# Second layer of a fused attention and MoE kernel: its first two chunks placed inside the w_out product, its second product two chunks behind, the last group ending with chunk 0

## Chip, cores and metric

The kernel runs on one core of a Trainium2 chip. The metric is the device time of that core in microseconds (us); lower is better. Engines are named TensorE (PE in the profile; PEld is its weight load), VectorE (DVE), ScalarE (ACT), GpSimd (POOL) and SyncE (SP, which issues DMA transfers).

## Reference

The attention part gives x, 2304 tokens of 512 values. Two layers follow. All inputs come in 64-bit floats.

```python
a = phi - np.max(phi, axis=2, keepdims=True); a = np.exp(a)
a = a / (np.sum(a, axis=2, keepdims=True) + 1e-09)
k_m = np.einsum('bhsm,bhsd->bhmd', a, k); v_m = np.einsum('bhsm,bhsd->bhmd', a, v)
scores = scale * np.matmul(q, k_m.transpose(0, 1, 3, 2))
attn = softmax(scores)                 # max, exp, sum + 1e-09
x = np.matmul(attn, v_m)               # (4, 8, 576, 64) -> (2304, 512)

h = np.maximum(np.maximum(x @ w1, x @ w2), x @ w3)   # 512 -> 768
y = h @ w_out                                        # 768 -> 512

h = y @ w_in                                         # 512 -> 2048
g = np.maximum(h, 0.0) + np.log1p(np.exp(-np.abs(h)))
out = g @ w_out2                                     # 2048 -> 512
```

## The kernel before

Every product is made of three matmuls in reduced-precision 32-bit floats: a value is split into a high part, cast by ScalarE (L160), and a rest, value minus high part, by VectorE or GpSimd (L168). The 64-bit inputs are converted on the chip by the class `Conv`: ScalarE scales the upper word (L196 with Prelu, called "slope", or L198 with Copy, called "bits"), VectorE shifts (L203) and joins the lower word (L204) and, for "bits" alone, puts the sign back (L207); then ScalarE casts the high part and GpSimd makes the rest (L168). Between load and conversion stand two buffers `raw` and two buffers `cg`.

The first layer runs in two passes of 1152 tokens (three chunks of 384). `phase_a(pp)` makes h, `phase_o(pp)` the product with w_out: 18 steps, one per chunk cc and block j of 128 hidden values, in the order 5, 0, 1, 2, 3, 4. A step is 12 matmuls (L685 to L687, 128x384) into four PSUM banks, out of a ring of six (`psm`). `hsplit` splits h two steps ahead, into a ring of four buffers: the high part hh on ScalarE, the rest hlo on the engine that a table names, which is VectorE for two of the 18 steps in the second pass and GpSimd for the others. After a chunk's last step, ScalarE casts the four banks to yb (L160) and VectorE makes their rests (L168); that frees the banks. So the next chunk finds two banks free and waits for the other two.

During `phase_o(1)` the weight blocks of the second layer are loaded and converted by `w2_steps`, blocks 0 to 3 by "slope". The second layer runs over 96 steps: four groups of four blocks of 128 hidden values, in each group six chunks ck of 384 tokens, in each chunk the four blocks. A step n has `m2in` (12 matmuls, L918, into one of two `pst` banks), `soft1` (e on VectorE L924, L by ScalarE's Softplus L926, m on VectorE L928), `soft2` (high part gh on ScalarE L160, rest gl on GpSimd L168) and `m2out` (9 matmuls, L961, 128x512, into three `acc` banks). At a chunk's last block, the sums go to o: copied in group 0, added on VectorE (L974) in later groups. In the last group the rows of o are stored by SyncE (L133), where a tile of 128 tokens is cut into up to three pieces by the token order of the output.

From the start of the second pass on, a scheduler fixes the order on each engine: it takes the instructions in the order of the program text and lets one that is ready sooner go ahead. `m2out(n-1)` is written behind `m2in(n)`. Two lines, L673 in `hsplit` and one in `dma`, set who makes a rest and where transfers are issued:

```python
        rest(C["hl"][6 * cc + j], lo, src, hi)
            with tc.issue_after(LOADED["plan"]):
```

`issue_after(i)` orders what is traced under it behind instruction i where both are on the same engine.

## Time and profile before

| | us |
|---|---|
| median of 3 runs | 723.62 (723.2 to 723.75) |
| the profiled execution | 723.56 |
| its span | 721.7 |
| w_out product of the second pass, about | 265 to 307 |
| second layer, steady stretch | 316.22 to 712.36 |
| last stretch | 712.36 to 721.75 |

The times that the rows give are counted from the span's start. In a timeline's row stand the start, the duration, engine, line, operation, output<-input, count, and in brackets how long the engine idled before it and which instruction released it. A row can hold several instructions run one behind the other. PEclk is the granted clock of TensorE as a share of full speed. A matmul's duration holds its way through the array, so the distance of two starts is the price of one.

### The profile page before, as it was taken

Reading aid. Unit: us, or ns where it says so; the run is one execution under the profiler, and the core shown is the slowest. Engines: PE = TensorE matmul, PEld = TensorE weight load, DVE = VectorE, ACT = ScalarE, POOL = GpSimd, SP = SyncE. Lnnn points to the kernel's source line nnn. Section 1 sums busy time; section 2 is a strip of 40 time slices with the busy share of each in tenths; the row PEclk is TensorE's granted clock in tenths of the full one; section 3 lists DMA queues with packets and bytes.
Section 4 is the critical chain, followed back from the end, with each engine's and each line's share of the span. In section 5 each row is a group of like instructions: output and inputs, shape, how many; then the busy total and the mean of one; then the engine's idle time right before and its main releaser. Section 6 shows DMA issues by size and latency. Waiting matters only on the chain. (4 is left out here: it accounts for less than half of the span.)

```text
span 721.7 us, 11376 instructions
## 1 busy us (share of the span) xinstructions
PE 683.8 (95%) x4216; PEld 606.2 (84%) x4216; DVE 416.9 (58%) x764; ACT 299.9 (42%) x640; POOL 269.8 (37%) x283
## 2 busy tenths in 40 slices
PE   4788999999889999989999999999999999999996
PEld 3475778988779999879989988998888989998984
DVE  4789787845799846842333784344873336333432
ACT  3556355565676625543233542223442224222221
POOL 2513053474493228712222542223542225212221
PEclk9799999999979999999999999999999999999999
DMA  9992996132162005410000240000330000011212
GB/s 240 268 271 77 245 286 196 64 120 76 51 198 91 1 2 161 131 59 1 0 1 1 87 132 15 1 0 19 105 111 1 1 1 0 1 45 44 69 47 61
DMA packets 57463, 59.19 MB, mean 82 GB/s; under 512 B 9792, under 2 KB 52288, under 8 KB 57408
## 3 DMA queue, kind: packets, MB, share of 16 engines
q1 hardware_dynamic: 57024, 58.34, 27.8%
q8 instruction: 33, 0.54, 0.3%
q10 hardware_dynamic: 384, 0.13, 0.1%
q14 instruction: 22, 0.18, 0.1%
HBM read 53.74 MB, written 4.72 MB: 81 GB/s over the span
## 5 line engine op out<-in xcount | busy, mean ns | idle before, releaser
L168 POOL TENSOR_TENSOR gl<-m,gh 128x384 fp32r<-128x384 f32 x96 | 101.0, 1054 | 255.0 <-ACT gh L160 238.6
L924 DVE TENSOR_SCALAR e<-pst 128x384 int32<-128x384 int32 x96 | 53.2, 555 | 135.5 <-PE pst L918 135.5
L926 ACT ACTIVATE L<-e 128x384 f32<-128x384 f32 x96 | 50.4, 525 | 185.5 <-DVE e L924 185.4
L961 PE MATMUL acc<-ol,gh 128*128 128x512 f32 x288 | 114.1, 396 | 0.0
L961 PE MATMUL acc<-oh,gh 128*128 128x512 f32 x288 | 113.6, 394 | 0.4 <-ACT gh L160 0.4
L918 PE MATMUL pst<-yb,ih 128*128 128x384 f32 x384 | 102.2, 337 | 0.0
L639 PE MATMUL psm<-ah,uh 128*128 128x288 f32 x288 | 88.6, 309 | 3.6 <-ACT ah L504 1.0
L639 PE MATMUL psm<-al,uh 128*128 128x288 f32 x288 | 86.9, 302 | 1.1 <-DVE al L168 1.0
L639 PE MATMUL psm<-ah,ul 128*128 128x288 f32 x288 | 86.2, 301 | 0.0
L928 DVE SCALAR_TENSOR_TENSOR m<-pst,L 128x384 f32<-128x384 f32 x96 | 53.4, 556 | 56.4 <-ACT L L926 56.4
L961 PE MATMUL acc<-oh,gl 128*128 128x512 f32 x288 | 82.8, 396 | 0.0
L160 ACT ACTIVATE gh<-m 128x384 fp32r<-128x384 f32 x96 | 50.0, 523 | 64.5 <-DVE m L928 63.2
L918 PEld LDWEIGHTS pst<-yb,ih 128*128 128x128 f32 x384 | 70.1, 188 | 3.5 <-DVE m L928 0.7
L918 PE MATMUL pst<-y0h,ih 128*128 128x384 f32 x192 | 65.7, 342 | 2.7 <-DVE m L928 2.6
L918 PE MATMUL pst<-y0l,ih 128*128 128x384 f32 x192 | 65.1, 339 | 0.0
L918 PE MATMUL pst<-y0h,il 128*128 128x384 f32 x192 | 65.1, 339 | 0.0
L918 PE MATMUL pst<-yb,il 128*128 128x384 f32 x192 | 64.4, 336 | 0.0
L639 PEld LDWEIGHTS psm<-ah,uh 128*128 128x128 f32 x288 | 55.3, 192 | 9.7 <-DVE h L649 2.6
L961 PEld LDWEIGHTS acc<-oh,gl 128*128 128x128 f32 x288 | 53.7, 188 | 11.3
L961 PEld LDWEIGHTS acc<-oh,gh 128*128 128x128 f32 x288 | 54.0, 188 | 10.2 <-ACT gh L160 0.9
L961 PEld LDWEIGHTS acc<-ol,gh 128*128 128x128 f32 x288 | 54.1, 188 | 9.1
L639 PEld LDWEIGHTS psm<-al,uh 128*128 128x128 f32 x288 | 55.8, 194 | 1.7 <-DVE al L168 1.7
(161 smaller groups left out, 1330.9 us busy)
## 6 DMA issues: line engine op xcount, KB each, us to landing
wraw<-in_moe_w_dram SPq DMA_DIRECT2D x66, 256.0 KB, 4.3
raw<-in_moe_w_in_dram SPq DMA_DIRECT2D x16, 512.0 KB, 3.7
raw<-in_moe_w_out_dram SPq DMA_DIRECT2D x16, 512.0 KB, 3.6
kvm<-in_k_dram SPq DMA_DIRECT2D x8, 512.0 KB, 7.7
kvm<-in_v_dram SPq DMA_DIRECT2D x8, 512.0 KB, 6.9
wor<-in_moe_w_out_dram SPq DMA_DIRECT2D x6, 512.0 KB, 4.1
ph<-in_phi_dram SPq DMA_DIRECT2D x8, 256.0 KB, 5.2
qn<-in_q_dram SPq DMA_DIRECT2D x4, 512.0 KB, 5.1
```

The costliest lines, as they stand in the source:

```text
L160: nc.scalar.activation(out=dst, in_=src, func=AF.Copy)
L168: return e.tensor_tensor(out=dst, in0=src, in1=hi, op=ALU.subtract)
L639: nc.tensor.matmul(x, l[:, t, ws], r[:, cs], start=(n == 0), stop=(n == 5))
L918: nc.tensor.matmul(hx, l[:, ds], r[:, cs], start=(n == 0), stop=(n == 3 * ND - 1))
L924: nc.vector.tensor_scalar(out=e.bitcast(I32), in0=hx.bitcast(I32), scalar1=0x7FFFFFFF, scalar2=None, op0=ALU.bitwise_and)
L926: nc.scalar.activation(out=L, in_=e, func=AF.Softplus, scale=-1.0)
L928: nc.vector.scalar_tensor_tensor(out=m, in0=hx, scalar=0.0, in1=L, op0=ALU.max, op1=ALU.add)
L961: nc.tensor.matmul(acc[0][t], l[:, t * P:(t + 1) * P], r, **kw)
```

## The change

- `hsplit` takes an engine: in pass 1 rests with cc + j odd are made by VectorE, the others by GpSimd, nine each.
- Blocks 2 and 3 of the second layer's weights are converted by "bits" in place of "slope", which adds four L207 steps on VectorE.
- The tiles of the softplus lie in a pool of their own; `m2in` and `soft1` of steps 0 and 1 are put at steps 10 and 12 of the w_out product, `soft2(0)` at step 12.
- `m2out(n-2)` is written behind `m2in(n)`.
- From step 2 on, loads are issued under `issue_after` of the last matmul of `m2in(2)`.
- The last group takes the chunks in the order 1 to 5, 0. In its last step the 128-token tiles go in the order of their number of pieces, the rest's matmuls between them; four stores follow, two on SyncE and two on ScalarE's queue.

```diff
-    def hsplit(cc, j):
+    def hsplit(cc, j, eng=None):
...
-        rest(C["hl"][6 * cc + j], lo, src, hi)
+        rest(eng or C["hl"][6 * cc + j], lo, src, hi)
...
+        eng = [None if pp == 0 else "dve" if (cc + j) % 2 else "pool" for cc, j in seq]
...
     for f in range(FG):
-        w2_steps(bg, 4 * f, f)
-    phase_o(1, bg)
...
+        w2_steps(bg, 4 * f, f, **({} if f < 2 else {"sgn": "bits"}))
+    s_p = pool(ctx, "soft", side="left")
...
+    seq = [(fg, ck, fi) for fg in range(NG2) for ck in [(x + fg // (NG2 - 1)) % (2 * NCH) for x in range(2 * NCH)]
+           for fi in range(FG)]
...
+    def front(n):
+        fg, ck, fi = seq[n]
+        hx, i = m2in(n, ck, fg * FG + fi)
+        soft1(n, hx)
+        return i
+
+    for n in range(2):
+        bg[10 + 2 * n].append(lambda n=n: front(n))
+    bg[12].append(lambda: soft2(0))
+    phase_o(1, bg)
...
-        for t in range(NTT):
+        ts, end = range(NTT), n == len(seq) - 1
+        if end:
+            ts = sorted(ts, key=lambda t: -len(rows(ck * CH + t * P)))
+        lows = []
+        for x, t in enumerate(ts):
             mm(gh, oh, t, start=(fi == 0), stop=False)
             mm(gh, ol, t, start=False, stop=False)
-        for t in range(NTT):
-            mm(gl, oh, t, start=False, stop=last)
+            if end and x:
+                lows.append(ts[x - 1])
+                mm(gl, oh, ts[x - 1], start=False, stop=True)
+        for t in ts:
+            if t not in lows:
+                mm(gl, oh, t, start=False, stop=last)
...
-                    for p0, n, r0, st in rows(ck * CH + t * P):
-                        dma(out=out[r0:r0 + (n - 1) * st + 1:st, :], in_=O[ck, t][p0:p0 + n])
...
+                    for x, (p0, k, r0, st) in enumerate(rows(ck * CH + t * P)):
+                        dma(nc.scalar if end and (x or t == 1) else nc.sync, out=out[r0:r0 + (k - 1) * st + 1:st, :],
+                            in_=O[ck, t][p0:p0 + k])
...
-    for n, (fg, ck, fi) in enumerate(seq):
-        hx = m2in(n, ck, fg * FG + fi)
-        if n:
-            soft2(n - 1)
-        soft1(n, hx)
+    for n in range(2, len(seq) + 2):
+        if n < len(seq):
+            i = front(n)
+            if n == 2:
+                LOADED["plan"] = i
+        if n <= len(seq):
+            soft2(n - 1)
         for fn in bg.get(n, ()):
             fn()
-        if n:
-            m2out(n - 1)
-    soft2(len(seq) - 1)
-    m2out(len(seq) - 1)
+        m2out(n - 2)
```

In the changed kernel e is L919, L is L921, m is L923, `m2in` L913, `m2out` L976 and the stores L131.

**Where the second chunk's banks are freed.** On VectorE, before, the end of the conversion of block 4 (L204, L207) and the rests of yb for the second chunk's first two banks stand so:

```order
L204 SCALAR_TENSOR_TENSOR cg<-raw,cg 128x512
L203 TENSOR_SCALAR cg<-cg 128x512
L207 SCALAR_TENSOR_TENSOR cg<-raw,cg 128x512
L204 SCALAR_TENSOR_TENSOR cg<-raw,cg 128x512
L207 SCALAR_TENSOR_TENSOR cg<-raw,cg 128x512
L168 TENSOR_TENSOR yb_3486<-psm,yb 128x384
L203 TENSOR_SCALAR cg<-cg 128x512
L168 TENSOR_TENSOR yb_3488<-psm,yb 128x384
```

In the changed kernel the same place reads:

```order
L204 SCALAR_TENSOR_TENSOR cg<-raw,cg 128x512
L207 SCALAR_TENSOR_TENSOR cg<-raw,cg 128x512
L168 TENSOR_TENSOR hlo<-h,hh 128x384
L919 TENSOR_SCALAR e<-pst 128x384
L168 TENSOR_TENSOR yb_3486<-psm,yb 128x384
L203 TENSOR_SCALAR cg<-cg 128x512
L923 SCALAR_TENSOR_TENSOR m<-pst,L 128x384
L204 SCALAR_TENSOR_TENSOR cg<-raw,cg 128x512
L168 TENSOR_TENSOR yb_3488<-psm,yb 128x384
```

A rest of h and e of step 0 stand ahead of the first bank's rest, and m of step 0 with a whole L204 step between the first and the second.

On ScalarE, before, from block 4's cast oh to the four casts of yb (`yb_3485` is the first bank's):

```order
L160 ACTIVATE oh_3988<-cg_4138 128x512
L160 ACTIVATE yb_3485<-psm_3644 128x384
L198 ACTIVATE cg_4354<-raw_4286 128x512
L160 ACTIVATE yb_3487<-psm_3645 128x384
L160 ACTIVATE yb_3489<-psm_3646 128x384
L160 ACTIVATE hh_3820<-h_3057 128x384
L160 ACTIVATE yb_3491<-psm_3647 128x384
```

In the changed kernel:

```order
L160 ACTIVATE oh_3983<-cg_4133 128x512
L160 ACTIVATE yb_3485<-psm_3647 128x384
L198 ACTIVATE cg_4352<-raw_4281 128x512
L921 ACT_TABLE_LOAD
L921 ACTIVATE L_3774<-e_3772 128x384
L160 ACTIVATE yb_3487<-psm_3648 128x384
L160 ACTIVATE yb_3489<-psm_3649 128x384
L160 ACTIVATE hh_3867<-h_3057 128x384
```

The table load and L of step 0 stand between the casts of the first and the second bank.

**Where the second layer's second product begins.** On TensorE, before, the end of the first `m2out` (`acc`) and what follows it:

```order
L961 MATMUL acc_3953<-oh,gh 128x512
L961 MATMUL acc_3953<-ol,gh 128x512
L961 MATMUL acc_3951<-oh,gl 128x512
L961 MATMUL acc_3952<-oh,gl 128x512
L961 MATMUL acc_3953<-oh,gl 128x512
L918 MATMUL pst<-y0h_2739,ih 128x384
L918 MATMUL pst<-y0h_2739,il 128x384
L918 MATMUL pst<-y0l_2740,ih 128x384
L918 MATMUL pst<-y0h_2866,ih 128x384
```

In the changed kernel:

```order
L976 MATMUL acc_3991<-oh,gh 128x512
L976 MATMUL acc_3991<-ol,gh 128x512
L976 MATMUL acc_3989<-oh,gl 128x512
L976 MATMUL acc_3990<-oh,gl 128x512
L976 MATMUL acc_3991<-oh,gl 128x512
L976 MATMUL acc_3989<-oh,gh 128x512
L976 MATMUL acc_3989<-ol,gh 128x512
L976 MATMUL acc_3990<-oh,gh 128x512
L976 MATMUL acc_3990<-ol,gh 128x512
```

Two blocks of `m2out` follow each other, where one stood, since one more `m2in` has gone ahead of them.

**The last stores.** On SyncE, before, the last seven stores, all of the last chunk, and the end:

```order
L133 DMA out_dram<-o_4830 64x512
L133 DMA out_dram<-o_4830 32x512 x2
L133 DMA out_dram<-o_4832 96x512
L133 DMA out_dram<-o_4832 32x512
L133 DMA out_dram<-o_4834 96x512
L133 DMA out_dram<-o_4834 32x512
L1022 UNCONDITIONAL_BRANCH
```

In the changed kernel the last rows of SyncE, of which two stores are the last chunk's, and then those of ScalarE:

```order
L131 DMA out_dram<-o_4866 96x512
L131 DMA out_dram<-o_4866 32x512
L131 DMA out_dram<-o_4108 32x512
L131 DMA out_dram<-o_4104 128x512
L1043 UNCONDITIONAL_BRANCH
```

```order
L921 ACTIVATE L<-e 128x384
L160 ACTIVATE gh<-m 128x384
L131 DMA out_dram<-o_4108 96x512
L131 DMA out_dram<-o_4106 128x512
L1043 UNCONDITIONAL_BRANCH
```

Of the last chunk's four stores two stand on either queue, two of them whole tiles of 128 rows.

## Rows read from the trace of the kernel before

**Rows 1.** Page, busy us (share of the span) x instructions of each engine.

```profile
PE 683.8 (95%) x4216; PEld 606.2 (84%) x4216; DVE 416.9 (58%) x764; ACT 299.9 (42%) x640; POOL 269.8 (37%) x283
```

**Rows 2.** Windows: us, busy PE PEld DVE ACT POOL, PEclk, DMA, GB/s.

```profile
268.76:295.54 26.78, 25.91 (x146) 24.75 (x144) 20.30 (x23) 14.33 (x28) 22.16 (x18) 1.00 0.44 137
286.01:298.44 12.43, 10.58 (x55) 8.97 (x54) 8.47 (x11) 7.11 (x15) 10.34 (x8) 1.00 0.50 158
298.44:316.22 17.78, 15.60 (x77) 14.86 (x78) 13.05 (x21) 9.21 (x17) 8.73 (x7) 0.90 0.40 122
312.54:316.05 3.51, 3.51 (x12) 3.51 (x13) 0.97 (x2) 1.49 (x3) 2.01 (x2) 0.53 0.15 61
316.22:712.36 396.14, 395.59 (x1972) 355.14 (x1971) 178.68 (x299) 125.54 (x238) 125.02 (x113) 1.00 0.11 32
712.36:721.75 9.39, 2.37 (x10) 1.61 (x9) 1.88 (x3) 0.40 (x1) 1.02 (x1) 0.83 0.29 84
```

**Rows 3.** Chain of waits, second layer: start us, us, engine, tile, line, count.

```profile
428.68 2.10 PE acc L961 x9
430.78 3.54 PE pst L918 x20
```

**Rows 4.** TensorE in 265 to 300: waits (total, times, longest), then a weight load.

```profile
PE psm L687 <- POOL hlo L168: 1.8, 3, 0.9
...
298.44 0.19 PEld L685 LDWEIGHTS psm<-hh,wo 128*128 128x128 f32 x1 [0.40 <-DVE yb L168]
```

**Rows 5.** TensorE's timeline behind the first softplus: start us, us, ..., [idle <-releaser].

```profile
312.54 0.69 PE L918 MATMUL pst<-y0h,ih 128*128 128x384 f32 x1 [2.17 <-DVE m L928]
```

**Rows 6.** Timelines of VectorE in the second pass, and GpSimd at one place.

```profile
219.33 0.54 DVE L168 TENSOR_TENSOR hlo<-h,hh 128x384 fp32r<-128x384 f32 x1
...
289.51 1.36 DVE L168 TENSOR_TENSOR hlo<-h,hh 128x384 fp32r<-128x384 f32 x1
...
291.74 0.68 DVE L207 SCALAR_TENSOR_TENSOR cg<-raw,cg 128x512 int32<-128x512 int32 x1
...
293.87 1.67 DVE L207 SCALAR_TENSOR_TENSOR cg<-raw,cg 128x512 int32<-128x512 int32 x1
296.61 0.56 DVE L168 TENSOR_TENSOR yb<-psm,yb 128x384 fp32r<-128x384 f32 x1 [1.07 <-ACT yb L160]
...
289.27 1.19 POOL L168 TENSOR_TENSOR hlo<-h,hh 128x384 fp32r<-128x384 f32 x1
```

**Rows 7.** ScalarE's timeline, from the second chunk's banks to the first softplus.

```profile
290.52 0.67 ACT L198 ACTIVATE cg<-raw 128x512 f32<-128x512 f32 x1 [1.28 <-POOL hlo L168]
...
295.57 0.63 ACT L160 ACTIVATE oh<-cg 128x512 fp32r<-128x512 f32 x1 [2.08 <-DVE cg L207]
...
297.04 0.86 ACT L160 ACTIVATE yb<-psm 128x384 fp32r<-128x384 f32 x2
...
309.32 1.28 ACT L926 ACT_TABLE_LOAD   x1
311.12 0.52 ACT L926 ACTIVATE L<-e 128x384 f32<-128x384 f32 x1 [0.52 <-DVE e L924]
```

**Rows 8.** Page, the costliest groups: the last step of the softplus.

```profile
L928 DVE SCALAR_TENSOR_TENSOR m<-pst,L 128x384 f32<-128x384 f32 x96 | 53.4, 556 | 56.4 <-ACT L L926 56.4
```

**Rows 9.** TensorE's timeline at the end of the kernel.

```profile
711.50 0.86 PE L961 MATMUL acc<-oh,gl 128*128 128x512 f32 x3
712.81 0.50 PE L961 MATMUL acc<-oh,gh 128*128 128x512 f32 x1 [0.44 <-ACT gh L160]
```

**Rows 10.** End of the kernel: timelines of VectorE and SyncE, and store landings.

```profile
714.74 1.88 DVE L974 TENSOR_TENSOR o<-o,acc 128x512 f32<-128x512 f32 x3 [2.60 <-PE acc L961]
...
715.46 3.45 SPq L133 DMA_DIRECT2D out_dram<-o  x7
...
out_dram<-o SPq DMA_DIRECT2D x2, 192.0 KB, 2.3
```

More of the change, by code (lines that the diff above doesn't have):

```diff
@@ L748, in phase_o @@
         seq = [(cc, jof(pp * NJ + x)) for cc in range(NCH) for x in range(NJ)]
-        hsplit(*seq[0])
-        hsplit(*seq[1])
+        eng = [None if pp == 0 else "dve" if (cc + j) % 2 else "pool" for cc, j in seq]
+        hsplit(*seq[0], eng[0])
+        hsplit(*seq[1], eng[1])
         main = []
         for n, a in enumerate(seq):
-            main.append(lambda a=a, n=n: (m1out(pp, *a), hsplit(*seq[n + 2]) if n + 2 < len(seq) else None))
+            main.append(lambda a=a, n=n: (m1out(pp, *a), hsplit(*seq[n + 2], eng[n + 2]) if n + 2 < len(seq) else None))
         run(main, bg)
@@ L895, in fused_kernel @@
     for f in range(FG):
-        w2_steps(bg, 4 * f, f)
-    phase_o(1, bg)
-    right.close()
-    psA_s.close()
-    b_p = pool(ctx, "bwork", side="right")
-    psx = pool(ctx, "psx", space=PSUM)
+        w2_steps(bg, 4 * f, f, **({} if f < 2 else {"sgn": "bits"}))
+    s_p = pool(ctx, "soft", side="left")
     G, acc, O = {}, {}, {}
@@ L917, in m2in @@
             for l, r in ((ih, yh), (il, yh), (ih, yl)):
-                nc.tensor.matmul(hx, l[:, ds], r[:, cs], start=(n == 0), stop=(n == 3 * ND - 1))
+                i = nc.tensor.matmul(hx, l[:, ds], r[:, cs], start=(n == 0), stop=(n == 3 * ND - 1))
                 n += 1
-        return hx
+        return hx, i.ins
     def soft1(n, hx):
-        e = b_p.tile([P, CH], F32, tag="e", name="e", bufs=2)
+        e = s_p.tile([P, CH], F32, tag="e", name="e", bufs=2)
         nc.vector.tensor_scalar(out=e.bitcast(I32), in0=hx.bitcast(I32), scalar1=0x7FFFFFFF, scalar2=None, op0=ALU.bitwise_and)
-        L = b_p.tile([P, CH], F32, tag="L", name="L", bufs=2)
+        L = s_p.tile([P, CH], F32, tag="L", name="L", bufs=2)
         nc.scalar.activation(out=L, in_=e, func=AF.Softplus, scale=-1.0)
-        m = b_p.tile([P, CH], F32, tag="m", name="m", bufs=2)
+        m = s_p.tile([P, CH], F32, tag="m", name="m", bufs=2)
         nc.vector.scalar_tensor_tensor(out=m, in0=hx, scalar=0.0, in1=L, op0=ALU.max, op1=ALU.add)
@@ L932, in soft2 @@
         m = G[n]
-        gh = b_p.tile([P, CH], F32R, tag="gh", name="gh", bufs=3)
-        gl = b_p.tile([P, CH], F32R, tag="gl", name="gl", bufs=3)
+        gh = s_p.tile([P, CH], F32R, tag="gh", name="gh", bufs=3)
+        gl = s_p.tile([P, CH], F32R, tag="gl", name="gl", bufs=3)
         cast("act", gh, m)
@@ L937, in soft2 @@
         G[n] = (gh, gl)
+    seq = [(fg, ck, fi) for fg in range(NG2) for ck in [(x + fg // (NG2 - 1)) % (2 * NCH) for x in range(2 * NCH)]
+           for fi in range(FG)]
+    GS = 2 * NCH * FG
+    def front(n):
[7 more added lines that the diff above has]
+    phase_o(1, bg)
+    right.close()
+    psA_s.close()
+    b_p = pool(ctx, "bwork", side="right")
+    psx = pool(ctx, "psx", space=PSUM)
     def rows(c0):
@@ L961, in mm @@
             nc.tensor.matmul(acc[0][t], l[:, t * P:(t + 1) * P], r, **kw)
-        for t in range(NTT):
+        ts, end = range(NTT), n == len(seq) - 1
[3 more added lines that the diff above has]
+        for x, t in enumerate(ts):
             mm(gh, oh, t, start=(fi == 0), stop=False)
             mm(gh, ol, t, start=False, stop=False)
-        for t in range(NTT):
-            mm(gl, oh, t, start=False, stop=last)
+            if end and x:
[4 more added lines that the diff above has]
+                mm(gl, oh, t, start=False, stop=last)
         if last:
-            for t in range(NTT):
+            for t in ts:
                 if fg == 0:
@@ L975, in m2out @@
                 if fg == NG2 - 1:
-                    for p0, n, r0, st in rows(ck * CH + t * P):
-                        dma(out=out[r0:r0 + (n - 1) * st + 1:st, :], in_=O[ck, t][p0:p0 + n])
-    seq = [(fg, ck, fi) for fg in range(NG2) for ck in range(2 * NCH) for fi in range(FG)]
-    GS = 2 * NCH * FG
+                    for x, (p0, k, r0, st) in enumerate(rows(ck * CH + t * P)):
+                        dma(nc.scalar if end and (x or t == 1) else nc.sync, out=out[r0:r0 + (k - 1) * st + 1:st, :],
+                            in_=O[ck, t][p0:p0 + k])
     bg = defaultdict(list)
```

## Prediction

> **What bounds the kernel now.** I read the busy shares first: TensorE is busy for 683.8 of 721.7 us, the next engine for 58% [rows 1]. So only what lets TensorE start a matmul earlier, or shortens what follows its last matmul, moves the time. The profiled execution took 723.56 us, its span 721.7; the median of the runs is 723.62. I count from 723.56.
>
> Next came the windows. In the steady stretch of the second layer, 316.22 to 712.36 us, TensorE is busy for 395.59 of 396.14 us at full granted clock [rows 2]. Nothing is to be had there. The change can act on two places: the w_out product of the second pass with the passage into the second layer (265 to 316 us), and the last 9 us.
>
> I then took the price of one matmul where nothing waits: 20 of the second layer's first product take 3.54 us, 0.176 each; 9 of its second take 2.10 us, 0.233 each [rows 3]. By that price 55 matmuls in 286.01 to 298.44 are 9.68 us of 12.43, so 2.75 us are lost there; 77 in 298.44 to 316.22 are 13.55 of 17.78, so 4.2 are lost there [rows 2]. The lines show where. In the product TensorE waits for the low rests of h on GpSimd (three waits, the longest 0.93 us) and, at 298.44, for a PSUM bank that the rests of yb on VectorE free [rows 4]. After the product it idles 2.17 us at 312.54, behind the first softplus, and the 12 matmuls that follow take 3.51 us at a granted clock of 0.53, the lower of the two levels (1.2 of 2.4 GHz): 1.4 us more than 12 x 0.176 [rows 2, 5].
>
> **The passage, with nothing late.** I set a fixed point: the fourth PSUM bank of the product's last chunk opening, 298.44 before. From it to the first matmul of the second layer's second product (316.22) there were 77 matmuls. In the new order there are 78: 54 of the product and 24 of m2in, since m2in(1) and most of m2in(0) have gone ahead of it. One m2in more than before is done by then, 12 x 0.176 = 2.11 us of work that need not be done later. So if the bank opens at X, the gain is 316.22 + 2.11 - X - 78 x 0.176 = 304.6 - X. Without any wait, X is 298.44, less the 2.75 lost, plus 16 m2in matmuls that move ahead of it (2.82), less 5 product matmuls that move behind it (0.88): 297.63. The gain would be 7.0 us. This is the upper bound, with the 2.17 idle, the low clock and the waits for GpSimd all gone.
>
> **When the bank opens.** The bank needs ScalarE's cast and VectorE's rest of yb. Both engines reach them after the second half of weight block 4. On VectorE that conversion's last step ended at 293.87 + 1.67 = 295.54 [rows 6]. The source queues the held loads behind a TensorE instruction, but the loads sit on SyncE, and in the new order the conversions of blocks 4 to 6 stand where they stood; I give the hold no effect, and this is where the change doesn't do what it says. From 268.76 to 295.54 VectorE is busy for 20.30 of 26.78 us, so 6.5 are idle [rows 2]. The change adds four more rests of h (0.54 us alone at 219.33, 1.36 at 289.51 beside GpSimd's row at 289.27) and four L207 steps of blocks 2 and 3, 0.68 to 1.67 each [rows 6]: 4 x 0.54 + 4 x 0.68 = 4.9 to 4 x 1.36 + 4 x 1.67 = 12.1. Against 6.5 idle that makes the conversion 0 to 5.6 late, but the idle lies in pieces, behind loads and ScalarE's steps, and not every added step meets one. Walking the ring of two raw tiles from load to ScalarE to VectorE gives about 1.0 later, with the row lengths nearer 0.68; I take 1.0 (296.5) and keep 0 to 3.
>
> From 296.5 on ScalarE does three steps, the cast of oh, that of yb for bank 1 and a cg step; before, they took from 295.57 to 297.04, 1.47 us [rows 7]. So they end at 298.0, bank 1's cast in their middle at about 297.4. Then, and this is new, the softplus table load stands between the first and the second yb cast: 1.28, and L(0) 0.52 [rows 7], to 299.85. VectorE adds m, 0.56 [rows 8], an L204 step taken at 0.68 like the L207 row, and the second yb rest, 0.56 [rows 6]: X = 301.7. Before, the same stretch from the conversion's end to the bank was 2.90; now it is 5.2. GpSimd is no part of it, and its load falls by eight rests. The gain is 304.6 - 301.7 = 2.9, of the 7.0. TensorE's waits for GpSimd and its 2.17 us are gone, and in their place it stands at the third bank (freed about 298.2, wanted at 295.5: 2.7 us) and again at the fourth (1.4).
>
> After an idle of 2.17 us the trace shows the clock at 0.53 for 3.51 us [rows 2, 5]. After an idle of 2.7 I expect the same once. Most falls on the 12 matmuls before the second wait, which it only shortens. I take 0.5 lost, bounds 0 and 2.8 (two such stretches). Small waits elsewhere, for the first chunk's rests behind an added L207 step, for the third chunk's behind block 6: 0.3, bounds 0 and 1. One of the nine rests goes into the phase ahead of the product; its 0.54 I count at 0, bounds -0.5 and 0.5. Passage: -2.9 + 0.5 + 0.3 = -2.1.
>
> The Trainium skill, "ScalarE: Activation LUTs", section "What ACT_TABLE_LOAD costs", counts a drain of 1380 ns beside the 1283 ns of a load. By it X would be 1.38 later and the time 1.4 us longer, about 720.9. The row at 311.12 [rows 7] doesn't show such a drain: L started 1.80 us after the load began, released by its own input.
>
> **Two chunks behind.** m2out(n-2) follows m2in(n), so TensorE has two blocks of work while a softplus runs. In the steady stretch the old order covers it but for 0.55 us in all (395.59 of 396.14 [rows 2]); I leave this at 0, bounds -0.5 and +1. At the end it counts. The block before the last ended 711.50 + 3 x 0.233 = 712.20, and the last began 712.81 [rows 9], behind gh. Now two blocks of 2.10 us stand over that chain: -0.6. The granted clock after it was 0.83 on average [rows 2]: -0.1.
>
> **The stores.** Before, VectorE's three last adds start at 714.74 and the seven stores on SyncE take 3.45 us to issue from 715.46 [rows 10], 0.49 each: the last starts at 718.42, and the window ends at 721.75 [rows 2]. Chunk 0 last needs four stores, on two queues, so the last is issued behind the third add, 714.74 + 1.88 = 716.62. With the same tail the gain is 721.75 - 718.42 - (721.75 - 716.65), thus 1.8. But the last store now is 256 KB and all four move at once; stores of 192 KB landed in 2.3 us. The same bytes in less time can cost up to 0.9. I take -1.3, bounds -0.9 and -1.8. ScalarE has nothing else to do by then, so its two issues are free.
>
> **Sum.** 723.56 - 2.1 - 0.6 - 0.1 - 1.3 = 719.46, said as 719.4.
>
> **Rivals.**
> - The forecast, the wait moves to the second chunk's banks: 717 to 721.5. For it: on both engines the order puts the load, L and m ahead of the second rest. Chance 0.55.
> - All hidden: VectorE's idle takes the added steps in full, and the conversion of block 4 even ends 2 us earlier than before, since ScalarE's cg step at 290.52, which waited 1.28 behind a rest of h on GpSimd [rows 7], starts sooner. X near 298.7 gives 5.9, the end 2.0: 715.7 or, at the bound of 7.0, 714.5. For it: the 6.5 us of idle. Against it: the load's 1.28 stands on the path all the same. Chance 0.17.
> - Only the end pays: the conversion ends at 299.4, X is 304.6, and the passage gives nothing and costs one low-clock stretch of 1.4: 723.56 + 1.4 - 2.0 = 723.0; with half of that delay 721.6. Chance 0.20.
> - Slower: VectorE becomes the bound of the product. If the rests take 1.36 and the L207 steps 1.67 [rows 6], the conversion ends 5.6 late, X is 306.3, the passage loses 1.7 and two low-clock stretches 2.8, the end gives 2.0: 726.1. It decides from X = 305.3, a conversion ending at 300.1. For it: the 1.36 row beside a busy GpSimd. Against it: GpSimd was busy 22.16 of 26.78 us [rows 2] and loses rests, so fewer meet. Chance 0.08.
>
> On the last rival the Trainium skill speaks: "SBUF — State Buffer", section "SBUF: two separate sides", says that a VectorE operation with two SBUF inputs and a GpSimd operation that reads SBUF hold one port pair by turns, the other blocked for a whole instruction. The rows of 0.54 and 1.36 agree with it; by it every rest moved to VectorE beside a GpSimd one saves nothing.
>
> **How the numbers follow.** Likeliest: 719.4. The range goes down to the case of all hidden and up past half of the third: 714.5 to 723.0, leaving out the slower case and the tails. About 0.2% (1.45 us) is what a measurement can tell from no change: faster means under 722.1. Forecast and all hidden (0.72) and under half of the third (0.08) are faster: 0.80. The rest of the third is within it: 0.12. Slower: 0.08.
>
> **What would show it.** Right: TensorE idle twice in the last chunk's opening (2 to 3 us, then 1 to 2), behind VectorE's yb rests; the table load between two yb casts; no idle of 2 us behind the first softplus; no wait for gh in the last block; last store issued within 0.5 us of the last add. Wrong: the idle at the third bank under 1 us (all hidden), rests of h near 1.4 us with the block 4 conversion ending after 299 (third, slower), or a table load much over 1.28.

## The result and the profile after

The changed kernel takes 717.0 us, median of 4 runs (716.22 to 717.18); the kernel before takes 723.68 (723.2 to 725.82). The ratio is 0.990, 95% interval 0.9879 to 0.9921: 6.7 us faster. The profiled execution took 716.22 us, its span is 714.1.

The page's first line still shows TensorE at 95%:

```profile
PE 677.5 (95%) x4216; PEld 604.9 (85%) x4216; DVE 419.5 (59%) x775; ACT 301.2 (42%) x640; POOL 260.1 (36%) x276
```

Beside [rows 1], TensorE is busy 6.3 us less for the same 4216 matmuls. Some of the time was thus never idle time in the profile of before. To see where it went, I cut the span at three matmuls that both kernels have: the first one of the second pass's w_out product, the first of the second layer's second product, and the last. One m2in more (12 matmuls, 2.11 us) lies ahead of the second cut now, so 2.11 is taken from before's third line and put to its second.

| stretch | before | after | difference |
|---|---|---|---|
| start to the product's first matmul | 265.02 | 264.84 | -0.18 |
| from there to the second product's first matmul (passage) | 51.20 + 2.11 | 50.27 | -3.04 |
| from there to the end of the last matmul (second layer) | 398.79 - 2.11 | 393.44 | -3.24 |
| from there to the end of the span (tail) | 6.7 | 5.55 | -1.15 |

The four differences sum to the 7.6 us between the two profiled spans; the medians are 6.7 apart.

The windows of the changed kernel (stretch, its us, busy PE PEld DVE ACT POOL, granted clock, DMA share, GB/s) show the passage in two halves and the low clock between them:

```profile
286.00:301.30 15.30, 13.06 (x65) 12.37 (x64) 13.53 (x18) 9.53 (x19) 8.72 (x7) 0.89 0.44 137
297.70:301.40 3.70, 3.67 (x13) 3.54 (x13) 2.27 (x5) 3.67 (x8) 0.89 (x2) 0.57 0.30 120
301.30:315.11 13.81, 13.81 (x80) 13.49 (x78) 13.19 (x20) 6.75 (x14) 7.29 (x6) 1.00 0.44 122
315.11:705.00 389.89, 389.89 (x1954) 352.91 (x1954) 176.66 (x299) 126.68 (x238) 122.67 (x113) 1.00 0.11 34
```

After 301.30 TensorE is never idle, to the last matmul. The 2.17 us behind the first softplus [rows 5] are gone and so is the wait for gh at the end [rows 9]. In their place stands one wait in the product. TensorE's timeline at the last chunk's third bank, at its fourth bank, and at the second product (start, us, engine, line, operation, idle before and its releaser):

```profile
295.14 0.34 PE L913 MATMUL pst<-y0l,ih 128*128 128x384 f32 x1
297.73 0.69 PE L685 MATMUL psm<-hh,wo 128*128 128x384 f32 x1 [2.24 <-DVE yb L168]
...
301.35 0.42 PE L685 MATMUL psm<-hh,wo 128*128 128x384 f32 x1
...
315.11 0.50 PE L976 MATMUL acc<-oh,gh 128*128 128x512 f32 x1
```

VectorE at the same place: the conversion of block 4 ends at 294.38 + 1.66 = 296.04, the first bank's rest of yb follows at 297.11, m stands between it and the second.

```profile
294.38 1.66 DVE L207 SCALAR_TENSOR_TENSOR cg<-raw,cg 128x512 int32<-128x512 int32 x1
...
297.11 0.56 DVE L168 TENSOR_TENSOR yb<-psm,yb 128x384 fp32r<-128x384 f32 x1
...
299.65 0.56 DVE L923 SCALAR_TENSOR_TENSOR m<-pst,L 128x384 f32<-128x384 f32 x1 [1.31 <-ACT L L921]
...
300.73 1.01 DVE L168 TENSOR_TENSOR yb<-psm,yb 128x384 fp32r<-128x384 f32 x2
```

ScalarE: the table load and L stand between the yb casts of the first bank (296.61) and the second (299.52).

```profile
296.61 0.47 ACT L160 ACTIVATE yb<-psm 128x384 fp32r<-128x384 f32 x1
...
297.80 1.28 ACT L921 ACT_TABLE_LOAD   x1
299.09 0.53 ACT L921 ACTIVATE L<-e 128x384 f32<-128x384 f32 x1
299.52 0.85 ACT L160 ACTIVATE yb<-psm 128x384 fp32r<-128x384 f32 x2
```

The tail: three adds, two stores on ScalarE's queue, and the landing of one of them.

```profile
708.29 1.88 DVE L997 TENSOR_TENSOR o<-o,acc 128x512 f32<-128x512 f32 x3 [3.87 <-PE acc L976]
...
709.01 1.57 ACTq L131 DMA_DIRECT2D out_dram<-o  x2
...
out_dram<-o ACTq DMA_DIRECT2D x1, 256.0 KB, 2.8
```

### The profile page after: what moved, and what is told of

It is laid out like the page before. It is cut to its first block, busy times and chain, and to the rows that moved or that the text cites. A ratio compares the mean times of both kernels' runs of the same rounds, so it can differ in the third digit from the quotient of the medians.

```text
span 714.1 us, 11371 instructions
## 1 busy us (share of the span) xinstructions
PE 677.5 (95%) x4216; PEld 604.9 (85%) x4216; DVE 419.5 (59%) x775; ACT 301.2 (42%) x640; POOL 260.1 (36%) x276
## 4 chain that ended last, share of the span: by engine, by line
PE 72%; DVE 11%; DMA 9%; issue 3%; ACT 3%; SPq 2%; DVEq 0%; ACTq 0%; POOL 0%
PE acc L976 28%; PE pst L913 28%; PE psm L639 7%; DMA qn<-in_q_dram 2%; DMA wraw<-in_moe_w_dram 2%; DMA wor<-in_moe_w_out_dram 2%; PE psm L685 2%; PE psm L686 2%; PE psm L687 2%; DVE cg L204 2%; SPq L133 1%; DVE cg L203 1%; DMA kvm<-in_k_dram 1%; DMA raw<-in_moe_w_out_dram 1%; DVE wh L204 1%
## 5 line engine op out<-in xcount | busy, mean ns | idle before, releaser
L919 DVE TENSOR_SCALAR e<-pst 128x384 int32<-128x384 int32 x96 | 53.3, 555 | 145.7 <-PE pst L913 145.7
L921 ACT ACTIVATE L<-e 128x384 f32<-128x384 f32 x96 | 50.3, 524 | 182.6 <-DVE e L919 182.5
L976 PE MATMUL acc<-ol,gh 128*128 128x512 f32 x288 | 113.4, 394 | 0.0
L976 PE MATMUL acc<-oh,gh 128*128 128x512 f32 x288 | 113.3, 394 | 0.0
L913 PE MATMUL pst<-yb,ih 128*128 128x384 f32 x384 | 106.2, 337 | 0.0
L923 DVE SCALAR_TENSOR_TENSOR m<-pst,L 128x384 f32<-128x384 f32 x96 | 53.5, 557 | 61.3 <-ACT L L921 61.3
L976 PE MATMUL acc<-oh,gl 128*128 128x512 f32 x288 | 81.9, 392 | 0.0
L913 PEld LDWEIGHTS pst<-yb,ih 128*128 128x128 f32 x384 | 70.2, 188 | 2.2
L913 PE MATMUL pst<-y0l,ih 128*128 128x384 f32 x192 | 64.8, 337 | 0.0
L976 PEld LDWEIGHTS acc<-oh,gl 128*128 128x128 f32 x288 | 54.1, 188 | 12.5
L913 PE MATMUL pst<-y0h,ih 128*128 128x384 f32 x192 | 64.6, 337 | 0.0
L913 PE MATMUL pst<-y0h,il 128*128 128x384 f32 x192 | 64.5, 336 | 0.0
L913 PE MATMUL pst<-yb,il 128*128 128x384 f32 x192 | 64.5, 336 | 0.0
L976 PEld LDWEIGHTS acc<-oh,gh 128*128 128x128 f32 x288 | 53.9, 187 | 8.8 <-DVE yb L168 0.2
L976 PEld LDWEIGHTS acc<-ol,gh 128*128 128x128 f32 x288 | 54.1, 188 | 8.3
```

What stands on the lines that cost most here:

```text
L913: i = nc.tensor.matmul(hx, l[:, ds], r[:, cs], start=(n == 0), stop=(n == 3 * ND - 1))
L919: nc.vector.tensor_scalar(out=e.bitcast(I32), in0=hx.bitcast(I32), scalar1=0x7FFFFFFF, scalar2=None, op0=ALU.bitwise_and)
L921: nc.scalar.activation(out=L, in_=e, func=AF.Softplus, scale=-1.0)
L923: nc.vector.scalar_tensor_tensor(out=m, in0=hx, scalar=0.0, in1=L, op0=ALU.max, op1=ALU.add)
L976: nc.tensor.matmul(acc[0][t], l[:, t * P:(t + 1) * P], r, **kw)
```

## The experiments

Three questions were open: what holds TensorE in the passage; where the 3.2 us in the second layer come from, for which the prediction had 0.7; and what makes the tail shorter. Single executions of one kernel scatter more than these terms: beside the experiments the kernel before ran from 718.8 to 727.4 us. So each experiment is read twice, by its median over 4 to 12 runs, and by the lengths of its own stretches in its profiled execution, cut as above.

The changed kernel itself ran again beside three of the experiments.

> The changed kernel once more, on the same chip as the next three, so that each is told against it: 717 us, the third bank of the last chunk some 33 us after the product's first matmul, the second layer's second product 50.3 us after it.

717.94 us (715.53 to 719.06). The second layer is the same to 0.05 us. The passage is 52.30 in place of 50.27, and TensorE's timeline shows why:

```profile
297.90 0.45 PE L685 MATMUL psm<-hh,wo 128*128 128x384 f32 x1 [2.26 <-DVE yb L168]
...
301.62 0.69 PE L685 MATMUL psm<-hh,wo 128*128 128x384 f32 x1 [0.73 <-DVE yb L168]
```

The window behind the second wait (columns as above):

```profile
302.00:306.00 4.00, 4.00 (x14) 4.00 (x14) 4.00 (x8) 2.00 (x5) 2.66 (x3) 0.50 0.40 131
```

The first wait is as long as before. But here the first eight matmuls behind it run at full clock; the clock falls at the ninth, TensorE still reaches the fourth bank early, waits for it again, and the clock stays at 0.5 until about 306. The fourth bank opened 36.5 us after the product's first matmul in both executions. In the first one the low clock lay on the 12 matmuls ahead of it, where TensorE would have waited anyway, and cost nothing; here it lies on 14 matmuls behind it and costs the 2 us.

Three kernels told below have the same order on every engine up to the second product. Their passages are 51.90, 51.45 and 51.62, and in the first two the clock does not fall in it at all. There block 4 is converted later: ScalarE starts its second half, behind the load, 27.9 to 28.3 us after the product's first matmul in place of 26.6, and in all five executions VectorE's conversion ends 4.4 to 4.6 us behind that. Why the load lands later is not shown. ScalarE's row in the changed kernel, then ScalarE's row and TensorE's two waits in the kernel with all stores on one queue, whose product starts at 264.35:

```profile
291.45 0.67 ACT L198 ACTIVATE cg<-raw 128x512 f32<-128x512 f32 x1 [1.50 <-DMA raw<-in_moe_w_out_dram]
```

```profile
292.61 0.68 ACT L198 ACTIVATE cg<-raw 128x512 f32<-128x512 f32 x1 [1.44 <-DMA raw<-in_moe_w_out_dram]
...
298.85 0.44 PE L685 MATMUL psm<-hh,wo 128*128 128x384 f32 x1 [2.25 <-DVE yb L168]
...
302.48 0.45 PE L685 MATMUL psm<-hh,wo 128*128 128x384 f32 x1 [1.27 <-DVE yb L168]
```

So the passage's gain is 1.0 to 3.0 us from execution to execution, 1.7 in the median of the five, against the one profiled execution of the kernel before.

**What holds TensorE in the passage.** Theory A: block 4's conversion stands ahead of the rests of yb on VectorE. Theory B: the table load stands between the yb casts on ScalarE. Theory C: VectorE has too much to do in the passage as a whole.

Block 4's conversion moved behind the second chunk's rests; `YR` holds the rests' instructions:

```diff
-                rest("dve", yl[:, cs], yps[0][dm], yh[:, cs])
+                YR[cc, dm] = rest("dve", yl[:, cs], yps[0][dm], yh[:, cs]).ins
...
+            def a(x=x):
+                with (tc.issue_after(YR[1, ND - 1]) if f == FG else ExitStack()):
+                    cv[f, x].a()
+
-            bg[s + gap * (1 + x)].append(lambda x=x: cv[f, x].a())
+            bg[s + gap * (1 + x)].append(a)
```

> VectorE's steps of block 4's conversion are put behind the four rests of yb of the second chunk; nothing else is changed. Theory A (that conversion, which ended at 296.04 in the changed kernel, sets when the third bank opens at 297.73): the casts and rests follow the second chunk's last matmul, the third bank opens at about 294.6, the idle of 2.24 us and the half clock behind it (1.4 us) go, the fourth bank opens at about 297.0 before it is wanted; 3 to 4 us faster than the changed kernel, about 713.3. Theory B (the softplus table load between the casts of the first and the second bank holds TensorE): it stands there still, the idle moves from the third bank to the fourth, gain under 1 us. Theory C (VectorE as a whole is too slow for the product): the conversions then hold the third chunk's rests and the idle comes at the first matmul of the second product, gain under 1 us.

718.86 us (717.45 to 720.49): no gain. TensorE's wait at the third bank is gone, as theory A has it, and a longer one stands in front of the second product. TensorE, and VectorE's rests of the third chunk that it waits for:

```profile
315.45 0.50 PE L980 MATMUL acc<-oh,gh 128*128 128x512 f32 x1 [3.75 <-DVE yb L168]
...
313.92 1.48 DVE L168 TENSOR_TENSOR yb<-psm,yb 128x384 fp32r<-128x384 f32 x3
```

Passage 51.64; and the low clock behind this wait lies beyond the cut, where it makes the second layer 1.6 us longer than the changed kernel's (columns as above):

```profile
316.00:320.00 4.00, 4.00 (x12) 3.12 (x11) 3.40 (x7) 2.02 (x4) 1.01 (x1) 0.57 0.47 133
```

Theory A is right on the place and wrong on the price: the conversions of blocks 4 to 6 pass the wait on to the next rests behind them. This is theory C. So all three blocks were moved out of the passage:

```diff
-                with (tc.issue_after(YR[1, ND - 1]) if f == FG else ExitStack()):
+                with (tc.issue_after(YR[NCH - 1, ND - 1]) if f >= FG else ExitStack()):
```

> VectorE's steps of the conversions of blocks 4, 5 and 6 are put behind the last rest of yb of the third chunk; nothing else is changed. Theory C (VectorE's work between the product's start and the second layer bounds the passage: moving block 4 alone only shifted the idle to the first matmul of the second product, 3.75 us): with all three blocks out of the passage neither idle is left; the second product begins some 47.5 us after the product's first matmul in place of 50.3, and the low-clock stretch goes with the idle: 2 to 3.5 us faster than the changed kernel, about 714. Rival (the six half conversions then delay e and m of the first steps of the second layer, which VectorE makes too): the gain is given back in waits of TensorE within the first 30 us of the second layer, within 1 us of the changed kernel.

714.49 us (713.22 to 714.91), against 717.94 of the changed kernel beside it: 3.4 faster, no run of the one among those of the other. VectorE's timeline, where the third chunk's rests now wait for ScalarE's casts of what TensorE has just made, and TensorE no longer waits for them, and the windows of the passage and of the first 31 us behind it:

```profile
308.75 2.12 DVE L168 TENSOR_TENSOR yb<-psm,yb 128x384 fp32r<-128x384 f32 x4 [6.94 <-ACT yb L160]
```

```profile
266.31:313.77 47.46, 46.72 (x267) 45.77 (x265) 30.56 (x47) 24.62 (x48) 21.18 (x17) 1.00 0.21 67
313.77:345.00 31.23, 31.23 (x157) 28.12 (x157) 18.77 (x31) 14.63 (x28) 14.69 (x12) 1.00 0.33 101
```

The passage is 47.46 us, at full clock. The rival fell too: VectorE does two of the six half conversions in the last 3 us of the passage and four in the next 31 us (18.77 us busy), TensorE has no idle time there, and the second layer is as long as the changed kernel's. Since two buffers hold the chain, most of the loads for these blocks leave the passage with VectorE's steps (DMA share 0.21, in place of 0.44 in the windows of the changed kernel); the experiment does not tell the two apart. The change's own hold does nothing: without its two lines the order on every engine comes out the same, since it queues transfers of SyncE behind an instruction of TensorE, and `issue_after` orders one engine alone.

Theory B was tried twice. First the load was put early, by a small Softplus at the product's second step:

```diff
-        w2_steps(bg, 4 * f, f, **({} if f < 2 else {"sgn": "bits"}))
+        w2_steps(bg, 4 * f, f, sgn="bits")
...
+    d = s_p.tile([P, 4], F32, name="d")
+    bg[1].append(lambda: nc.scalar.activation(out=d, in_=ones, func=AF.Softplus))
```

> A small Softplus at the product's second step takes the table load out of the place between the yb casts; blocks 0 and 1 are converted by bits too, since Prelu would need the old table, which adds four L207 steps on VectorE. Theory A (block 4's conversion sets the third bank, and the 12 matmuls behind the idle run at half clock for 3.6 us, longer than the fourth bank needs): within 0.7 us of the changed kernel, the idle at the third bank as it was or up to 1 us longer by the added steps. Theory B (the load holds the fourth bank, 1.28 us and L of 0.53): 1.5 to 2 us faster, about 715.2.

724.4 us (721.31 to 727.56), slower than either theory has it. TensorE's timeline has two longer waits in the product; VectorE's has two rests of h that take 3.21 us together:

```profile
281.84 0.44 PE L685 MATMUL psm<-hh,wo 128*128 128x384 f32 x1 [1.04 <-DVE yb L168]
...
301.20 0.69 PE L685 MATMUL psm<-hh,wo 128*128 128x384 f32 x1 [2.65 <-DVE yb L168]
...
291.19 3.21 DVE L168 TENSOR_TENSOR hlo<-h,hh 128x384 fp32r<-128x384 f32 x2
```

The passage is 53.51, 1.2 to 3.2 us longer than the changed kernel's: with four L207 steps more, block 4's conversion ends 35.4 us after the product's first matmul, in place of 31.1 to 32.8. From that end to the second bank's rest it is 1.6 us here and 5.2 to 5.4 with the load between the casts. So the load does hold the fourth bank, as theory B has it, but what that gives back is less than the later conversion takes. This experiment changed two things; a third that it changed by chance is told below. Its profiled execution was the fastest of 12 (721.31), so what made the median 3 us more is not in these rows. Then steps 0 and 1 were put later, which moves the load behind all four casts with nothing added:

```diff
-        bg[10 + 2 * n].append(lambda n=n: front(n))
-    bg[12].append(lambda: soft2(0))
+        bg[13 + 2 * n].append(lambda n=n: front(n))
+    bg[15].append(lambda: soft2(0))
```

> The second layer's steps 0 and 1 are put at steps 13 and 15 of the product in place of 10 and 12; the table load then stands behind all four yb casts. Theory A: the third bank opens at about 297.6 as before, but 18 fewer matmuls of m2in stand ahead of it, so TensorE idles some 5.5 us there; from the bank 66 product and 42 m2in matmuls follow, 108 x 0.175 = 18.9 us, and the second product begins at about 316.6 in place of 315.1: 1.0 to 1.8 us slower than the changed kernel. Theory B (the load is what holds the banks): 2 us faster.

717.66 us (716.01 to 718.01); passage 52.00, in the range of the changed kernel's own (50.27 to 52.30). Theory B's 2 us did not come, though the fourth bank was open when TensorE came to it. Theory A's idle at the third bank did not come either: TensorE waited before it, 2.51 us for a rest of h that stands behind block 3's conversion on VectorE.

```profile
291.73 0.96 PE L687 MATMUL psm<-hlo,wo 128*128 128x384 f32 x4 [2.51 <-DVE hlo L168]
...
288.77 2.90 DVE L168 TENSOR_TENSOR hlo<-h,hh 128x384 fp32r<-128x384 f32 x2
```

Again VectorE's queue, at another row of it. Two parts of the change load or relieve VectorE, and each was undone alone. The bits, which add four steps:

```diff
-        w2_steps(bg, 4 * f, f, **({} if f < 2 else {"sgn": "bits"}))
+        w2_steps(bg, 4 * f, f)
```

> Blocks 2 and 3 are converted by slope again, which takes the four added L207 steps from VectorE; all else as in the changed kernel. Theory C (VectorE's work up to the second chunk's rests of yb bounds the passage): four steps, together 4.1 us in the changed kernel's trace, stand less before the gate; the third bank opens 1 to 3 us earlier and the time falls by as much against the changed kernel, 714.5 to 717. Rival (the conversions keep to the pace of the loads and of ScalarE, and VectorE only fills that): within 0.7 us.

717.15 us (715.7 to 718.3): no difference, the rival's result. Block 4's conversion did end earlier, 30.2 us after the product's first matmul in place of 31.2. But ScalarE then took a cg step ahead of the yb cast, and the first bank's rest came 32.4 us after the product's start, as in the changed kernel (32.3 in its first execution):

```profile
293.54 1.66 DVE L207 SCALAR_TENSOR_TENSOR cg<-raw,cg 128x512 int32<-128x512 int32 x1
...
297.42 0.54 DVE L168 TENSOR_TENSOR yb<-psm,yb 128x384 fp32r<-128x384 f32 x1
...
295.98 0.67 ACT L198 ACTIVATE cg<-raw 128x512 f32<-128x512 f32 x1
```

So theory C holds in this form: it is not the sum of VectorE's work that binds, but what stands ahead of the rests of yb, and the conversions of blocks 4 to 6 need not stand there. These conversions themselves keep to the landing of their loads, as the five executions above show. The alternation of the rests of h:

```diff
-        eng = [None if pp == 0 else "dve" if (cc + j) % 2 else "pool" for cc, j in seq]
+        eng = [None] * len(seq)
```

> The rests of h go back to the old table, two on VectorE and sixteen on GpSimd; all else as in the changed kernel. Theory A (VectorE's conversion of block 4 is the gate, and four rests of 0.56 to 1.46 us each stand before it): the conversion ends 1 to 2 us earlier, TensorE waits for GpSimd's rests before (some 1.8 us, as in the kernel before) come out of the idle at the third bank; 0 to 1.5 us faster than the changed kernel. Rival (the alternation is what took the 1.8 us of waits for GpSimd away): 1.5 to 2.5 us slower.

719.49 us (718.55 to 721.75), 0.9952 of the kernel before with an interval of 0.9926 to 0.9978; the changed kernel did not run beside it. The passage is 52.02, with 0.72 of wait for GpSimd and the wait at the bank as ever:

```profile
301.69 0.44 PE L685 MATMUL psm<-hh,wo 128*128 128x384 f32 x1 [2.10 <-DVE yb L168]
```

The profiled execution took 721.19 us, and in it the product began at 268.11, against 263.7 to 266.3 in the other kernels with this change. The medians are on the rival's side: 719.49 is 1.5 to 2.5 us above the changed kernel's two medians (717.0 and 717.94). But the rows put that ahead of the product, where one rest goes back to GpSimd, and not on the waits for GpSimd; whether that rest or chance makes the product start late is open. In the passage an effect of the alternation, if any, is smaller than the scatter of 2 us.

**The second layer.** Its 3.24 us are 0.7 at the end (the wait for gh, [rows 9]) and 2.5 that the prediction did not have. Either the order (m2out two steps behind) or the place of the softplus tiles, which moved to another pool, could bring them. The order undone:

```diff
+    soft2(1)
+    m2out(0)
-    for n in range(2, len(seq) + 2):
+    for n in range(2, len(seq)):
...
-        m2out(n - 2)
+        m2out(n - 1)
+    soft2(len(seq) - 1)
+    m2out(len(seq) - 1)
```

> The second product is written one step behind again, m2out(n-1) behind m2in(n); all else as in the changed kernel. If the two steps' distance made the steady stretch faster: blocks of 9 and 12 matmuls break up as in the kernel before, single waits of 0.4 us come back and gh is waited for in the last step, 1.5 to 2.5 us slower. If the price of one matmul of the second product (231.1 ns in place of 233.3) comes from the tiles of the softplus lying elsewhere: that price stays at 231, and only the wait at the end comes back, 0.5 to 1 us slower.

723.23 us (721.05 to 726.45), against 717.94: 5.3 slower, more than either expectation, and the wait for gh in the last step, which both expected, did not come back. The second layer is 6.9 us longer than the changed kernel's. TensorE's waits in it (us in total, times, longest) and one of them in the timeline, while the next group's weights are converted:

```profile
PE pst L913 <- DVE m L923: 4.4, 3, 2.2
PE acc L976 <- ACT gh L160: 0.5, 1, 0.5
```

```profile
428.67 0.44 PE L913 MATMUL pst<-y0h,ih 128*128 128x384 f32 x1 [1.88 <-DVE m L923]
```

These waits are 4.9 us; behind the longest of them, at 527.97, the clock is low once more (columns as above), some 1.7 us:

```profile
529.00:533.00 4.00, 4.00 (x14) 3.57 (x13) 2.65 (x5) 1.63 (x4) 1.04 (x2) 0.57 0.29 103
```

Two steps' distance is worth all of that in this kernel. It is not the order of the kernel before: here `soft1(n)` is written ahead of `soft2(n-1)`, there behind it, and the conversions fall differently among VectorE's steps. The kernel before lost less to one step's distance, 1.7 us: 0.6 at 419.7 us, 0.4 at 521.0, 0.7 at 712.8. The first of them, in the kernel before:

```profile
419.67 0.44 PE L918 MATMUL pst<-y0h,ih 128*128 128x384 f32 x1 [0.44 <-DVE m L928]
```

That leaves some 1.5 of the 3.24, and the place of the tiles. In the kernel before, e, L, m, gh and gl begin 32 bytes beyond a multiple of 64 bytes in each partition; in the changed kernel at a multiple of 64. A tile of 32 bytes in the kernel before moves them alone:

```diff
         if n:
             m2out(n - 1)
+        if n == 1:
+            pad = b_p.tile([P, 8], F32, name="pad")
+            nc.vector.memset(pad, 0.0)
```

> The kernel before, with a tile of 32 bytes per partition put behind the softplus tiles, so that e, L, m, gh and gl begin 32 bytes lower, at multiples of 64 bytes, as they do in the changed kernel; one small memset on VectorE is added. If the place of these tiles sets the price: a matmul of the second product costs 231.1 ns in place of 233.3, 864 x 0.0022 = 1.9 us faster than the kernel before. If the order of the blocks sets it: no change.

724.53 us (722.8 to 726.65), against 723.93 of the kernel before beside it; ratio 1.0007, interval 0.9992 to 1.0021. No gain in time. The price did change, as the chain of waits shows (start, us, engine, tile, line, count): first this kernel, then the changed kernel, then the kernel with the early load, whose tile `d` of 16 bytes had moved the softplus tiles to 32 bytes beyond a multiple of 64 again.

```profile
443.20 2.08 PE acc L961 x9
```

```profile
484.84 2.08 PE acc L976 x9
```

```profile
484.69 2.10 PE acc L978 x9
```

The median over all unbroken blocks of 9 is 231.1 ns a matmul in this kernel, in the changed one and in every experiment whose tiles begin at a multiple of 64 bytes; it is 233.3 in the kernel before and in the one with the early load. 864 x 0.0022 = 1.9 us. The kernel with the early load shows it in time: its second layer is 395.4 us long in place of 393.4, and in neither does TensorE wait in it. With the 1.7 of the waits that makes 3.6 for a difference of 3.24; the 0.4 between is not accounted for.

In the kernel before with the added tile the second layer was 1.4 us shorter than in the profile of before. 1.05 of it was given back ahead of it, behind the first softplus, where the wait was 3.22 us in place of 2.17 [rows 5]. ScalarE's rows show why:

```profile
313.15 0.62 PE L918 MATMUL pst<-y0h,ih 128*128 128x384 f32 x1 [3.22 <-DVE m L928]
...
310.68 1.28 ACT L926 ACT_TABLE_LOAD   x1 [1.98 <-DVE e L924]
311.98 0.52 ACT L926 ACTIVATE L<-e 128x384 f32<-128x384 f32 x1
```

In the kernel before the table load ran before e was made, and L began 0.52 us behind the load, released by e [rows 7]; here the load itself waits for e. So this edit moved the load as well, whether by the memset or by the tiles' place is open. The price by place is shown, and its worth in the second layer; that it brings the whole program 1.9 us is not.

**The tail.** All four stores on one queue:

```diff
-                        dma(nc.scalar if end and (x or t == 1) else nc.sync, out=out[r0:r0 + (k - 1) * st + 1:st, :],
+                        dma(nc.sync, out=out[r0:r0 + (k - 1) * st + 1:st, :],
```

> All four stores of the last chunk go through SyncE; chunk 0 is still the last. If the second queue is worth something: the last issue comes up to 0.7 us later and the stretch from the last matmul to the end grows from 5.55 us to 5.8 to 6.3. If four stores in place of seven are the whole gain: 5.55 again.

717.23 us (715.89 to 718.87), tail 5.69, between the two expectations; passage 51.90. And the old order of chunks with two queues:

```diff
-    seq = [(fg, ck, fi) for fg in range(NG2) for ck in [(x + fg // (NG2 - 1)) % (2 * NCH) for x in range(2 * NCH)]
+    seq = [(fg, ck, fi) for fg in range(NG2) for ck in [x for x in range(2 * NCH)]
```

> The last group takes the chunks in the old order, so that chunk 5 with its seven stores is last, on two queues; all else as in the changed kernel. If the number of stores sets the end: three more issues of 0.49 us over two queues, the stretch from the last matmul to the end grows from 5.55 us by 0.5 to 0.8, against 6.7 in the kernel before. If the bytes set it: 5.55 again.

717.07 us (715.87 to 719.1), tail 5.88, 0.33 more than 5.55 and less than the 0.5 to 0.8 that the number of stores would have cost; passage 51.45. ScalarE's queue has five of the seven. The issues of the one and of the other:

```profile
710.16 1.76 SPq L131 DMA_DIRECT2D out_dram<-o  x4
```

```profile
709.47 2.59 ACTq L131 DMA_DIRECT2D out_dram<-o  x5
```

Together with [rows 10] these make a square: seven stores on one queue 6.7, seven on two 5.9, four on one 5.7, four on two 5.5 to 5.6. Either half of the edit alone gives most of the 1.15 us; the other then adds 0.1 to 0.3. The issue time of seven stores on one queue was the cost, as the prediction had it, and either half takes most of it away.

The last kernel joins the conversions moved out of the passage with the last step's matmuls kept in the order in which the change writes them (the scheduler had put the three rests' matmuls last all the same):

```diff
-            nc.tensor.matmul(acc[0][t], l[:, t * P:(t + 1) * P], r, **kw)
+            with (tc.issue_after(PM[-1]) if end and PM else ExitStack()):
+                i = nc.tensor.matmul(acc[0][t], l[:, t * P:(t + 1) * P], r, **kw)
+            if end:
+                PM.append(i.ins)
```

> The kernel with the conversions of blocks 4 to 6 behind the third chunk's rests of yb, and in the last step the matmuls kept in the order of the text, so that the rest's matmul of the first tile stands four places ahead of the last matmul and that of the second one place. The passage as in that kernel (second product 47.5 us behind the product's first matmul). Two of the three adds then run beside the last matmuls: the stretch from the last matmul to the end falls from 5.55 us to 4.6 to 5.0; 713.8 against 714.5. If the bytes of the stores set the end, it stays at 5.5.

712.27 us (711.23 to 713.68); the kernel before beside it 724.57; ratio 0.9829, interval 0.9808 to 0.9851. The passage is 47.73, the tail 5.10, just outside the 4.6 to 5.0 expected and well under the 5.5 that the bytes alone would have set. The adds now begin 0.7 us before the last matmul has ended (704.34 + 2 x 0.23 = 704.80):

```profile
704.09 1.97 DVE L1004 TENSOR_TENSOR o<-o,acc 128x512 f32<-128x512 f32 x3 [3.42 <-PE acc L981]
```

It beats the kernel before by 12 us, and the changed kernel, which did not run beside it, by some 4.7 (717.0).

## Why the prediction was right, and where it was not

The sum was -4.1 us, the measured change is -6.7. 717.0 lies in the range, at the lower edge of the forecast's own case (717 to 721.5). The mechanism of the passage was right; one term was missed, and without its 2.5 us the time would have been near the likeliest 719.4.

- **The third and the fourth bank.** Forecast: block 4's conversion 1.0 later than before, third bank about 298.2, wait 2.7, X = 301.7. Measured: 0.7 later counted from the product's start, 297.73, wait 2.4, X = 301.35. From the conversion's end to the bank it is 5.2 us, as forecast. The working stands. The second wait, forecast at 1.4, is 0 in the first execution, where the low clock fills its time, 0.73 in the second, and 1.27 and 1.22 in the two executions where the clock does not fall.
- **The clock.** The term of 0.5 with bounds of 0 and 2.8 was the loosest: 0 in the first profiled execution, some 2 us in the second, by where the low-clock stretch falls. The end of block 4's conversion scatters too, by 1.7 us, inside the bounds of 0 to 3 that the prediction kept for it. The passage's gain is 1.0 to 3.0, and the forecast of 2.1 lies near its middle; that the first profiled execution shows the best of it, 3.0, is luck.
- **The hold.** No effect, as forecast.
- **Two chunks behind.** This is the step that failed: "I leave this at 0, bounds -0.5 and +1", read from a busy share of 395.59 of 396.14 us [rows 2]. The second layer gained 2.5 us more than the 0.7 at its end. The busy share did not show it, because a matmul that starts late behind its neighbour, or costs 233.3 ns in place of 231.1, counts as busy. The two waits at 419.7 and 521.0 us, 1.0 together, stand in the timeline of before and were waved through with that share. The price itself was taken from the same trace [rows 3], so what the tiles' place costs was in it already and could not be seen there at all; for the move of the tiles to a pool of their own the prediction has no term.
- **The end.** gh's wait is gone (forecast -0.7), the stores gave -1.15 (forecast -1.3, bounds -0.9 and -1.8). The expression for the gain "with the same tail" has its sign reversed as written, 3.33 - 5.10; the size of 1.8 is right.
- **All hidden, the first rival.** It did not happen, and the kernel with the conversions moved out shows what it is worth: a passage of 47.5 against the 46.3 that the bound of 7.0 meant.
- **The slower rival.** VectorE's queue is what binds the passage, but more by the rows' places than by their number: four added steps less changed nothing (717.15). With four more the conversion ends 2.6 to 4.3 us later and the kernel takes 724.4 us, of which 2.0 by the tiles' place; that is this rival's mechanism. The prediction counts eight rests less on GpSimd; the pages show seven (283 and 276 instructions), which no term used.

The Trainium skill, "ScalarE: Activation LUTs", section "What ACT_TABLE_LOAD costs", counts a drain of about 1.38 us with each load. The changed kernel shows this place with an input that was ready (e ended at 296.98): load at 297.80, 1.28 us, L at 299.09. There is no such drain here, and the measurement decides.

## What to carry to other kernels

When an engine off the critical path frees the buffers of the one that is on it, look at what stands ahead of the freeing instruction in its queue, and move what isn't needed soon behind the last such instruction, not behind the first: the latter only moves the wait. An ordering hint is worth nothing on an engine that doesn't issue the work; look in the built order whether it did anything. A busy share near 100% bounds the idle time and not the price of one instruction: where an engine is full, that price is what is left to look at.

## What the runs showed of the hardware

A matmul of 128x512 whose stationary operand lay in a tile that begins at a multiple of 64 bytes in its partition took 231.1 ns, one whose tile began 32 bytes further 233.3, each in the order of blocks of the kernel before and in that of the changed kernel. All five tiles of the softplus moved together, so which of them counts wasn't told apart; gh and gl are those that TensorE reads.

After the same wait of 2.24 to 2.26 us at the same instruction, the granted clock was at the lower of its two levels at once in one execution (the first matmul 0.69 us, the next ones 0.32 apart) and only after some 1.5 us in another (the first 0.45, the next seven 0.17 apart, then 0.32). In two more (the kernels with one queue and with chunk 5 last) it stayed at full through that wait and through the next one of 1.2 to 1.3 us.
